# Smaller last loads, held-back loads, a cut last store and a separate last wait in a channel-attention kernel on one core

## Chip, cores and metric

The kernel runs on one core of one Trainium2 chip. The metric is the device time of one execution in microseconds; the median of the runs counts. One execution is recorded by the hardware profiler; its times are in the profile.

## What is computed

The input `x` has 1 x 384 x 384 x 384 bf16 elements (113 MB) and `w1d` has one weight (k = 1).

```python
g = jnp.einsum("bhwc->bc", x) / (H * W)      # mean of each channel over all pixels
s = _sigmoid(g * w1d[0])                      # one factor per channel
return x * s[:, None, None, :]
```

Every element is needed twice: once for the mean, before any output is known, and once to be scaled.

## The kernel before

**Layout.** The 147456 pixels are spread over the 128 partitions, 1152 rows of pixels for each partition; a row is 384 channels, 768 bytes in each partition. SBUF holds one large tile, `arena` (275 rows for each partition). "A load of n rows" brings 128 partitions x n rows.

**First pass.** The whole input is loaded once, 1152 rows. TensorE sums every row into one PSUM bank with a matrix of ones (`sum_rows`, line 272, issuing from L261). Some groups of rows stay on the chip until the second pass: some as they are ("raw"), others packed by VectorE into fewer rows (`fold`, L295 and L301, with a test on ScalarE at L332), and a few in PSUM. `N_STREAM` rows are not kept and are loaded again in the second pass. The last things loaded in the first pass are raw rows, by `take_raw` (line 466): `V`, the `LATE` pieces, `W`, `T` and `Y`. `T` and `Y` are scratch of `fold` until then. After the last row's matmul, ScalarE takes the sigmoid (L475), which gives `s_bf`.

**Second pass.** VectorE multiplies rows by `s_bf` in place (`scale`, L487; a few pieces on GpSimd), and the rows are stored (`store`, L499). Kept groups are unpacked first (`unfold`). As stores land, the rows they held come free, and rows of the stream are loaded into them (`load`, L255).

**Who sets the order.** All transfers but one tiny one are issued by SP, in one order, and the engine of each instruction waits by semaphores that `Flow` (line 21) derives from the rows read and written. SP works strictly in order: a load that waits for a store to land holds all that SP issues after it. The order of the second pass is found while the kernel is built, by a small planner (the `while True` loop at line 723). It keeps a clock `now`, a list of transfers under way (`moves`), and the free rows (`idle`; `runs()` lists the free stretches). `backlog()` is the time that the queued transfers will still take. A load is issued into the longest free stretch as soon as this line allows it:

```python
if (todo or not (landed or alongside or waiting)) and (n >= BIG or n == left or (ahead < LOW and n >= 8) or ahead < LAST):
```

Here `n` is the length of the stretch, cut to what is left, `ahead` the backlog in microseconds, `BIG` 32 rows, `LOW` 9 and `LAST` 4.

**The end.** `Flow.emit` puts everything into one critical section (`tile_critical`), and at its end SP waits for the last transfer of each of its 24 semaphore lanes (L126). Leaving the section, all engines meet; then the kernel's own end follows (L830).

Of the kernel before, what the change touches and what calls it, by code (L numbers as in the profile page):

```python
# [20 lines left out]
class Flow:  # L21
# [47 lines left out]
    def emit(self):  # L69
        nc = self.nc  # L70
        engines = {"SP": nc.sync, "ACT": nc.scalar, "PE": nc.tensor, "DVE": nc.vector, "POOL": nc.gpsimd}

        know = {e: {} for e in engines}

        def covers(k, d):
            return k.get(d.lane, 0) >= d.rank if d.dma else k.get(d.eng, -1) >= d.i

        for s in self.steps:
            k = know[s.eng]
            for d in sorted(s.deps, key=lambda d: -d.i):  # L80
                if covers(k, d):
                    continue
                s.waits.append(d)
                d.wanted = True
                for key, v in d.know.items():
                    if k.get(key, -1) < v:
                        k[key] = v
            s.know = dict(k)
            if s.dma:
                s.know[s.lane] = s.rank  # L90
            else:
                s.know[s.eng] = s.i

        count, sems = {}, {}
        for s in self.steps:
            if not s.dma and s.wanted:
                s.rank = count[s.eng] = count.get(s.eng, 0) + 1

        def sem(s):
            key = s.lane if s.dma else s.eng  # L100
            if key not in sems:
                name = f"f_{key[0]}{key[1]}" if s.dma else f"f_{key}"
                sems[key] = self.tc.alloc_semaphore(name)
            return sems[key]

        last = {}
        with self.tc.tile_critical():  # L107
            for s in self.steps:
                eng = engines[s.eng]
                waits = [(sem(d), d.rank * (16 if d.dma else 1)) for d in s.waits]  # L110
                hold = None if s.dma or s.bare or not waits else waits.pop()
                for h, v in waits:
                    eng.wait_ge(h, v)
                ins = s.emit()
                if ins is None:
                    continue
                if hold:
                    ins = ins._wait_ge(*hold)
                if s.dma:
                    ins.then_inc(sem(s), 16)  # L120
                    last.pop(s.lane, None)
                    last[s.lane] = s
                elif s.wanted:
                    ins.then_inc(sem(s), 1)
            for lane, s in last.items():
                engines[lane[0]].wait_ge(sem(s), 16 * s.rank)  # L126


@with_exitstack
def kernel(  # L130
# [11 lines left out]
    nc = tc.nc  # L142
    P = nc.NUM_PARTITIONS
    B, H, W, C = x.shape
# [16 lines left out]
    V = G0 + PAIRS * 3 * PAIR  # L161
    A = V + PAIR
    N_A = 39
    T = A + N_A
    Y = T + 2 * PIECE
# [14 lines left out]
    W = A + 3 * PIECE  # L180
# [13 lines left out]
    arena = pool.tile([P, ROWS, C], bf16, name="arena")  # L194
# [13 lines left out]
    of = out.rearrange("b h w c -> (b h w) c")  # L208
# [4 lines left out]
    def view(t, r0, n):  # L213
        return t[r0 * P : (r0 + n) * P, :].rearrange("(p r) c -> p r c", r=n)
# [193 lines left out]
    for i, bk in enumerate(banks):  # L408
        lo, hi = i * BANK, min((i + 1) * BANK, PS * C)
# [31 lines left out]
    LATE = [(W + 4, 8), (U, 8), (W + 12, 8), (W + 20, 7)]  # L441
# [8 lines left out]
    left = first - N_FIRST  # L450
# [15 lines left out]
        load(raw(a), a, n)  # L466
        sum_rows(a, n)

    for a, n in [(V, 8), *LATE, (W, 4), (T, 8), (Y, 4), (Y + 4, 3), (Y + 7, 1)]:
        take_raw(a, n)  # L470
    assert summed[0] == RPP

# [17 lines left out]
            reads=rows(a, n) + ["s_bf" if s is s_bf else "bank0"], writes=rows(a, n), after=after,  # L490
        )

    def store(at, a, n):
        r0, m = run = run_of(at)
        lo, hi = at - r0, at - r0 + n
        assert hi <= m
        return fl.add(
            "SP",
            lambda: nc.sync.dma_start(out=view(of, *run)[:, lo:hi, :], in_=arena[:, a : a + hi - lo, :]),  # L499
            reads=rows(a, hi - lo), dma=True,  # L500
        )

    def unfold(k, first):

# [88 lines left out]
    ROW, PER_LOAD, PER_STORE = 0.2267, 0.112, 0.061  # L593
    LAT, SEEN, DT = 2.0, 1.5, 0.05
    PENDING, MERGE = 24.0, 12.0
    BIG, CAP, PART, LOW, LAST = 32, 48, 16, 9.0, 4.0
    BANKS_AT = 2
    N_SPLIT = 2
    now = dve_at = 0.0
    moves, waiting, over, acts = deque(), deque(), deque(), deque()  # L600
    landed = deque()
    idle = [False] * ROWS
    todo = 0
# [35 lines left out]
    def stored(a, n):  # L639

        def f():
            for i in range(a, a + n):
                unused.discard(i)
                if not Y <= i < Y + 8:
                    idle[i] = True
        return f
# [8 lines left out]
    alongside = deque()  # L655
# [17 lines left out]
    since = None  # L673
    asked = checked = False
    stall = 0.0

    def start_group():

# [44 lines left out]
    while True:  # L723

        if dve_at <= now:
            ahead = backlog()
            can = bool(turns)
            if not can and not alongside and (ahead >= PENDING or not landed):
                can = start_group()
            if landed and (ahead < PENDING or not can):  # L730
                a, at, n, end = landed.popleft()
                scale(a, n, s=s_ps if alongside and now else s_bf)
                dve_at = now + TT(n)
                since = (a, at) if since is None else since
                if end or ahead < MERGE:
                    b, first = since
                    send(first, b, at + n - first, stored(b, at + n - first))
                    since = None
            elif can:
                f, t, then = turns.popleft()  # L740
                f()
                dve_at = now + t
                if then:
                    then()
        if alongside and alongside[0][0] <= now:
            _, a, at, n = alongside.popleft()
            store(at, a, n)
            moves.append([now + LAT, n * ROW + PER_STORE, stored(a, n)])
        while waiting and waiting[0][0] <= now:
            _, n, then, at, a, known = waiting.popleft()  # L750
            known.append(store(at, a, n))
            moves.append([now + LAT, n * ROW + PER_STORE, then])
        if not asked and not line and not turns:
            verdict()
            asked = True
        if out_rows == total and not checked:
            checked = True
            fl.add("POOL", again, reads=["odd_i", "s_bf"], writes=rows(Y, N_OVER), after=written, bare=True)
        while over and over[0][0] <= now:
            over.popleft()[1]()  # L760

        got = runs()
        if bank_at is None and len(line) <= total - BANKS_AT and got and max(got)[0] >= N_BANKED:
            a = max(got)[1]
            for i in range(a, a + N_BANKED):
                idle[i] = False
            back = arena[:, a : a + PS, :].rearrange("p r c -> p (r c)")
            for i, bk in enumerate(banks):
                lo, hi = i * BANK, min((i + 1) * BANK, PS * C)
                copy_bank(bk[:, 0 : hi - lo], back[:, lo:hi], [("bank", i)], rows(a, PS))  # L770
            for lo, hi, at, cell in PARTS:
                copy_bank(at, arena[:, a + N_BANKED - 1, lo:hi], [], rows(a + N_BANKED - 1, 1) + [cell])
            bank_at = (a, now + 5.0)
            got = runs()

        if got and todo < N_STREAM:
            n, a = max(got)
            left = N_STREAM - todo
            left -= run_of(left - 1)[0]
            n = min(n, CAP, left)  # L780
            ahead = backlog()
            if (todo or not (landed or alongside or waiting)) and (n >= BIG or n == left or (ahead < LOW and n >= 8) or ahead < LAST):

                lo = N_STREAM - todo - n
                load(lo, a, n)
                for i in range(a, a + n):
                    idle[i] = False
                parts = [(a + e, lo + e, f - e, f == n) for e, f in split(n, PART)]
                todo += n
                moves.append([now + LAT, n * ROW + PER_LOAD, lambda parts=parts: landed.extend(parts)])  # L790

        if moves and moves[0][0] <= now:
            moves[0][1] -= DT
            if moves[0][1] <= 0:
                over.append((now + SEEN, moves.popleft()[2]))
        else:
            stall += DT
        if not (alongside or moves or waiting or over or landed or line or turns) and todo == N_STREAM:
            break
        now += DT  # L800
# [34 lines left out]
```

## Time and profile before

| | us |
|---|---|
| runs | 720.6, 720.0, 720.54 |
| median | 720.54 |
| profiled execution, its own time | 720.05 |
| its span (first to last instruction of the record) | 718.3 |

| engine | busy us | share of the span |
|---|---|---|
| VectorE (DVE) | 485.6 | 68% |
| TensorE (PE) | 213.0 | 30% |
| ScalarE (ACT) | 122.1 | 17% |
| GpSimd (POOL) | 10.2 | 1% |
| DMA queue of SP, share of 16 engines' span | | 98.9% |

The page gives busy times over the whole span, cut into 40 slices of 18 us. PE and ACT work almost only in the first 270 us, the summing pass; DVE works in both. The windows view cuts any stretch of the span into pieces of its own. In it a row is: window in us, its length, then busy time of PE, PE weight load, DVE, ACT and POOL (with the count of instructions that overlap it), the granted TensorE clock, the share of the 16 DMA engines that is busy, and the GB/s that they move. A share slightly over 1 comes from transfers that are counted where they begin. In the timeline view a row is: start in us, duration, engine, line, operation, and in brackets the idle time before it and what ended it.

### The profile page before, as it was taken

To read this page: it belongs to the slowest core of one execution; us is meant where nothing else is said; L and a number is where in the kernel's file an instruction comes from. 1 tells how busy PE (TensorE), PEld (TensorE's weight loads), DVE (VectorE), ACT (ScalarE), POOL (GpSimd) and SP (SyncE) were. 2 spreads that over 40 slices of the span, in tenths; PEclk is the share of its full clock that TensorE was granted. 3 is DMA by queue.
4 is the path that set the end of the run, shared out by engine and by line. 5 is a ranking of instruction groups with operands and counts; after the bars stand their busy time and mean duration, and the time that the engine had idled before them with its cause. 6 is when DMAs were issued, how large, how long until landed. Compare 5 with 4: busy or idle time off the path is not lost.

```text
span 718.3 us, 2042 instructions
## 1 busy us (share of the span) xinstructions
PE 213.0 (30%) x1186; PEld 0.3 (0%) x3; DVE 485.6 (68%) x454; ACT 122.1 (17%) x101; POOL 10.2 (1%) x7
## 2 busy tenths in 40 slices
PE   4776977997868770000000000000000000000000
PEld 0000000000000000000000000000000000000000
DVE  4606270639896819998997999996991999005640
ACT  3604160426674610000002000000000000000000
POOL 0000000000000005000000000000000000000000
PEclk9989889999999995555555555555555555555555
DMA  9999999999999989999999999999999999999997
GB/s 372 443 422 444 434 431 418 447 428 424 428 426 428 425 343 359 413 424 430 425 434 429 433 443 424 435 426 437 434 431 432 443 431 426 436 429 431 447 421 307
DMA packets 21181, 303.30 MB, mean 422 GB/s; under 512 B 2354, under 2 KB 2738, under 8 KB 9010
## 3 DMA queue, kind: packets, MB, share of 16 engines
q1 hardware_dynamic: 21168, 303.18, 98.9%
q8 instruction: 4, 0.07, 0.0%
q14 instruction: 7, 0.06, 0.0%
q10 hardware_dynamic: 2, 0.00, 0.0%
HBM read 189.92 MB, written 113.25 MB: 422 GB/s over the span
## 4 chain that ended last, share of the span: by engine, by line
DMA 54%; DVE 27%; PE 7%; ACT 3%; another core or an unknown queue 2%; POOL 1%; SPq 1%; issue 1%; DVEq 0%; ACTq 0%
DMA arena<-in_x_dram 38%; DVE arena L487 19%; DMA out_dram<-arena 16%; PE bank L261 7%; DVE arena L295 6%; DVE arena L301 3%; ACT arena L332 2%; POOL arena L487 1%; SPq L255 1%; ACT arena L405 1%; SPq L499 0%; ACT s_bf L475 0%; ACT bank L479 0%; ACT bank L405 0%
## 5 line engine op out<-in xcount | busy, mean ns | idle before, releaser
L487 DVE TENSOR_TENSOR arena<-arena,s_bf 128x1536 bf16<-128x1536 bf16 (+9 forms) x100 | 231.0, 2345 | 84.4 <-DMA arena<-in_x_dram 68.2
L261 PE MATMUL bank<-arena,ones 128*128 128x384 bf16 x1151 | 207.1, 341 | 46.7 <-DMA arena<-in_x_dram 46.2
L295 DVE TENSOR_SCALAR arena<-arena 128x1536 uint16<-128x1536 uint16 (+3 forms) x240 | 142.9, 644 | 111.4 <-DMA arena<-in_x_dram 94.9
L332 ACT ACTIVATE arena<-arena 128x3072 uint16<-128x3072 uint16 (+1 forms) x40 | 108.0, 2700 | 111.0 <-DVE arena L295 111.0
L301 DVE TENSOR_TENSOR arena<-arena 128x1536 uint16<-128x1536 uint16 (+2 forms) x100 | 109.3, 1093 | 7.9 <-PE bank L261 4.0
L557 PE MATMUL bank<-odd,ones 128*128 128x1 bf16 x1 | 0.2, 185 | 313.8 <-DVE odd L552 313.8
L405 ACT COPY arena<-bank 128x512 uint32<-128x512 uint32 (+3 forms) x9 | 4.4, 497 | 107.9 <-DMA out_dram<-arena 107.6
L487 POOL TENSOR_TENSOR arena<-arena,s_bf 128x1536 bf16<-128x1536 bf16 (+1 forms) x3 | 10.0, 3351 | 269.4 <-ACT bank L479 269.4
L487 DVE TENSOR_TENSOR arena<-arena,bank 128x1536 bf16<-128x1536 bf16 (+3 forms) x8 | 9.4, 1250 | 0.0
L405 ACT COPY bank<-arena 128x512 uint32<-128x512 uint32 (+3 forms) x9 | 4.1, 494 | 26.3 <-PE bank L261 26.2
L332 ACT ACTIVATION_READ_ACCUMULATOR arena<-arena 128x1 f32 x40 | 7.5, 186 | 0.0
L261 PE MATMUL bank<-zeros,ones 128*128 128x384 bf16 x32 | 5.5, 326 | 0.0
L475 ACT ACTIVATE s_bf<-bank,w_sc 128x384 bf16<-128x384 f32 x1 | 0.6, 580 | 13.9 <-PE bank L261 13.9
L275 PE MATMUL bank<-arena,ones 128*128 128x384 bf16 x1 | 0.5, 477 | 7.2 <-DMA arena<-in_x_dram 7.2
L803 ACT ACT_TABLE_LOAD x1 | 1.3, 1283 | 0.7 <-PEq L819 0.7
L362 DVE TENSOR_SCALAR w_sc<-bank 128x1 f32<-128x1 f32 x1 | 0.2, 159 | 1.1 <-PE bank L357 1.1
L352 DVE MEMSET ones<- 128x128 bf16 x1 | 0.2, 165 | 1.0 <-SPq L107 1.0
L357 PE MATMUL bank<-w_bf,ones 1*128 1x1 bf16 x1 | 0.2, 178 | 2.2 <-DMA w_bf<-in_w1d_dram 2.2
L557 PEld LDWEIGHTS bank<-odd,ones 128*128 128x128 bf16 x1 | 0.1, 103 | 572.9 <-DVE odd L552 572.9
L561 DVE CAST odd_i<-bank 128x1 int32<-128x1 f32 x1 | 0.2, 157 | 0.3 <-PE bank L557 0.3
L479 ACT COPY bank<-s_bf 128x192 uint32<-128x192 uint32 x1 | 0.3, 323 | 0.0
L547 DVE TENSOR_REDUCE worst<-seen 128x1 f32<-128x40 f32 x1 | 0.2, 188 | 0.0
(8 smaller groups left out, 0.9 us busy)
## 6 DMA issues: line engine op xcount, KB each, us to landing
arena<-in_x_dram SPq DMA_DIRECT2D x16, 4608.0 KB, 29.9
out_dram<-arena SPq DMA_DIRECT2D x9, 3072.0 KB, 24.1
out_dram<-arena SPq DMA_DIRECT2D x5, 4608.0 KB, 35.8
arena<-in_x_dram SPq DMA_DIRECT2D x7, 2304.0 KB, 19.8
arena<-in_x_dram SPq DMA_DIRECT2D x14, 1152.0 KB, 17.0
arena<-in_x_dram SPq DMA_DIRECT2D x5, 3072.0 KB, 15.2
arena<-in_x_dram SPq DMA_DIRECT2D x18, 768.0 KB, 8.9
arena<-in_x_dram SPq DMA_DIRECT2D x2, 4512.0 KB, 29.4
```

The costliest lines, as they stand in the source:

```text
L255: lambda: nc.sync.dma_start(out=arena[:, a : a + hi - lo, :], in_=view(xf, *run)[:, lo:hi, :]),
L261: return pe.add_instruction(mybir.InstMatmult(name=nc.get_next_instruction_name(), ins=[pe.lower_ap(rhs), pe.lower_ap(ones[:])], outs=[pe. ...
L275: return nc.tensor.matmul(acc, lhsT=ones[:], rhs=arena[:, i, :], start=first, stop=last)
L295: lambda: nc.vector.tensor_scalar(out=dst, in0=src, scalar1=s0, scalar2=s1, op0=op0, op1=op1),
L301: "DVE", lambda: nc.vector.tensor_tensor(out=dst, in0=a, in1=b, op=op), reads=reads, writes=writes
L332: lambda: nc.scalar.activation(out=y, in_=y, func=ACTF.Copy, accum_out=seen[:, 2 * k + i : 2 * k + i + 1]),
L405: "ACT", lambda: nc.scalar.copy(dst.bitcast(u32), src.bitcast(u32)), reads=reads, writes=writes
L475: lambda: nc.scalar.activation(out=s_bf[:], in_=acc, func=ACTF.Sigmoid, scale=w_sc[:, 0:1]),
L479: "ACT", lambda: nc.scalar.copy(s_ps.bitcast(u32), s_bf[:].bitcast(u32)), reads=["s_bf"], writes=["bank0"]
L487: lambda: vec.tensor_tensor(out=v, in0=v, in1=s[:, None, :].to_broadcast([P, n, C]), op=Op.mult),
L557: lambda: nc.tensor.matmul(votes, lhsT=ones[:], rhs=odd[:], start=True, stop=True),
L803: nc.scalar.preload_act_table(ACTF.Sigmoid)
```

## The change

Four edits, all to the order and the cutting of transfers:

1. The last loads of the first pass: `T` in two loads of 4 rows in place of one of 8, `Y` in 4, 2, 2 rows in place of 4, 3, 1.
2. The planner holds a load back while three things hold together: a store was issued since the last load (`storing`), fewer than `MANY` = 32 rows are free in all, and the backlog is at least `SHORT` = 5 us. In the order that results, the first eight loads of the second pass stay as they were, and later ones differ in size and place; the last loads are of 48, 48, 8 and 43 rows where they were of 48, 36, 22 and 43.
3. The last store (output rows at `at` = 0, 43 rows) is cut: its first `N_LAST` = 6 rows go as three transfers of 13, 51 and 64 partitions, the other 37 rows as one transfer of all partitions.
4. The wait for the transfer issued last is taken out of the list of 24 and put into a critical section of its own, after the first.

```diff
@@ Flow.emit
-            for lane, s in last.items():
-                engines[lane[0]].wait_ge(sem(s), 16 * s.rank)
+            ends = list(last.values())
+            for s in ends[:-1]:
+                engines[s.eng].wait_ge(sem(s), 16 * s.rank)
+        with self.tc.tile_critical():
+            engines[ends[-1].eng].wait_ge(sem(ends[-1]), 16 * ends[-1].rank)
@@
-    for a, n in [(V, 8), *LATE, (W, 4), (T, 8), (Y, 4), (Y + 4, 3), (Y + 7, 1)]:
+    for a, n in [(V, 8), *LATE, (W, 4), (T, 4), (T + 4, 4), (Y, 4), (Y + 4, 2), (Y + 6, 2)]:
         take_raw(a, n)
@@
-    def store(at, a, n):
+    def store(at, a, n, p0=0, p1=P):
...
-            lambda: nc.sync.dma_start(out=view(of, *run)[:, lo:hi, :], in_=arena[:, a : a + hi - lo, :]),
+            lambda: nc.sync.dma_start(
+                out=view(of, *run)[p0:p1, lo:hi, :], in_=arena[p0:p1, a : a + hi - lo, :]
+            ),
...
+    def store_last(at, a, n):
+        for p0, p1 in zip(LAST_CUTS, LAST_CUTS[1:]):
+            store(at, a, N_LAST, p0, p1)
+        return store(at + N_LAST, a + N_LAST, n - N_LAST)
@@ planner
+    MANY, SHORT = 32, 5.0
+    N_LAST, LAST_CUTS = 6, (0, 13, 64, P)
+    storing = True
...
             store(at, a, n)
+            storing = True
...
-            known.append(store(at, a, n))
+            known.append((store if at else store_last)(at, a, n))
+            storing = True
...
-            if (todo or not (landed or alongside or waiting)) and (n >= BIG or n == left or (ahead < LOW and n >= 8) or ahead < LAST):
+            behind = storing and sum(m for m, _ in got) < MANY and ahead >= SHORT
+            if not behind and (todo or not (landed or alongside or waiting)) and (n >= BIG or n == left or (ahead < LOW and n >= 8) or ahead < LAST):
+                storing = False
```

## Prediction

> **What bounds the kernel now.** I read the page's slices first, then the queue table, then windows of busy time over the second half, over the hand-over between the two passes, and over the last microseconds.
>
> ```profile
> DMA  9999999999999989999999999999999999999997
> GB/s 372 443 422 444 434 431 418 447 428 424 428 426 428 425 343 359 413 424 430 425 434 429 433 443 424 435 426 437 434 431 432 443 431 426 436 429 431 447 421 307
> q1 hardware_dynamic: 21168, 303.18, 98.9%
> HBM read 189.92 MB, written 113.25 MB: 422 GB/s over the span
> ...
> 290.00:712.00 422.00, 0.18 (x1) 0.10 (x1) 319.25 (x233) 4.37 (x9) 0.00 (x0) 0.50 1.01 432
> ```
>
> The DMA engines bound it. The last row (window; busy time of PE, weight load, DVE, ACT, POOL; clock; DMA share; GB/s) says that from 290 to 712 us they have no idle time: share 1.01, 432 GB/s, while DVE is busy 319 of 422 us. So an edit in this stretch gains only if it removes bytes, and an order of loads and stores can only lose, by leaving the engines empty. Three places are not full: the first slice, slices 15 and 16 (343 and 359 GB/s, where the summing pass ends and the scaling pass begins) and the last (307). The change touches the last two.
>
> A row of the arena is 128 x 768 B = 98.3 KB, so 0.228 us at 432 GB/s. The 21168 packets are 147 transfers of 144: 128 data packets, 8 for each of 16 engines, and one closing packet for each engine.
>
> The hand-over:
>
> ```profile
> 262.00:264.00 2.00, 1.83 (x12) 0.00 (x0) 0.00 (x0) 0.00 (x0) 0.00 (x0) 1.00 0.99 411
> 264.00:266.00 2.00, 1.16 (x9) 0.00 (x0) 0.00 (x0) 0.00 (x0) 0.00 (x0) 1.00 0.85 337
> 266.00:268.00 2.00, 2.00 (x13) 0.00 (x0) 0.00 (x0) 0.00 (x0) 0.00 (x0) 1.00 0.20 76
> 268.00:270.00 2.00, 0.75 (x5) 0.00 (x0) 0.60 (x2) 0.90 (x2) 0.20 (x1) 1.00 0.00 0
> 270.00:272.00 2.00, 0.00 (x0) 0.00 (x0) 2.00 (x3) 0.00 (x0) 2.00 (x1) 0.82 0.53 197
> ...
> 263.20 1.95 PE L261 MATMUL bank<-arena,ones 128*128 128x384 bf16 x11 [0.17 <-DMA arena<-in_x_dram]
> 265.99 2.76 PE L261 MATMUL bank<-arena,ones 128*128 128x384 bf16 x16 [0.84 <-DMA arena<-in_x_dram]
> 268.78 0.58 ACT L475 ACTIVATE s_bf<-bank,w_sc 128x384 bf16<-128x384 f32 x1 [13.93 <-PE bank L261]
> ```
>
> PE stands 0.84 us until the 8-row load into T has landed, then runs the last 16 rows (8, 4, 3, 1) without a wait, 2.76 / 16 = 0.173 us each, and the sigmoid starts at its end. The last loads land while PE is still behind: here PE ends last, not DMA.
>
> The end:
>
> ```profile
> 712.00:712.50 0.50, 0.00 (x0) 0.00 (x0) 0.00 (x0) 0.00 (x0) 0.00 (x0) 0.50 0.46 198
> 712.50:713.00 0.50, 0.00 (x0) 0.00 (x0) 0.00 (x0) 0.00 (x0) 0.00 (x0) 0.50 0.16 66
> 713.00:713.50 0.50, 0.00 (x0) 0.00 (x0) 0.00 (x0) 0.00 (x0) 0.00 (x0) 0.50 0.01 0
> 713.50:714.00 0.50, 0.00 (x0) 0.00 (x0) 0.00 (x0) 0.00 (x0) 0.00 (x0) 0.50 0.31 132
> 714.00:714.50 0.50, 0.00 (x0) 0.00 (x0) 0.00 (x0) 0.00 (x0) 0.00 (x0) 0.50 0.00 0
> 714.50:715.00 0.50, 0.00 (x0) 0.00 (x0) 0.00 (x0) 0.00 (x0) 0.00 (x0) 0.50 0.15 66
> 715.00:715.50 0.50, 0.00 (x0) 0.00 (x0) 0.00 (x0) 0.00 (x0) 0.00 (x0) 0.50 0.15 66
> 715.50:718.30 2.80, 0.00 (x0) 0.00 (x0) 0.00 (x0) 0.00 (x0) 0.00 (x0) 0.50 0.00 0
> ...
> L126 SPq EVENT_SEMAPHORE x12: 17/28/28, 692.2 to 716.7; - x12
> SPq L830 <- PEq L830: 0.8, 2, 0.6
> ```
>
> Packets count in the window where they start. The last store moves 43 x 768 = 33 KB packets. After 713.5 there are four: two (132 GB/s x 0.5 us = 66 KB), then one and one. Their time, 0.31 x 16 x 0.5 = 2.48 us for two, is 1.24 us each: 27 GB/s, a sixteenth of the full rate. So two of the 16 engines are not slow but late, by about 3 us, and end near 716.4, when the other fourteen, whose last packets start by 712.5, end at about 713.2 in the middle. Then SP's last wait passes at 716.7 and the span ends at 718.3.
>
> **The change part by part.** *Last loads 4, 4, 4, 2, 2.* Before, T lands at 265.95. Now its first half lands 4 x 0.228 = 0.91 us sooner, at 265.04; PE is free at 263.20 + 1.95 = 265.15 and sums it by 265.84; the second half is there at about 266.0 (one closing packet more) and summed by 266.7. Y's four rows land at 266.9, summed by 267.6; two more at 267.4, summed by 267.95; the last two at about 267.9, summed by 268.3. PE ended at 268.75: -0.45 us. PE now waits for DMA at nearly every piece, so I take -0.4. Bounds: 0, if splitting delays each landing by as much as it saves, and -0.55, when PE ends 0.35 us after the last landing. One more load is issued on SP; the engines have queued work then (share 0.99), which hides it. The whole second pass is a full queue behind the sigmoid, so this goes through to the end.
>
> *Load behind a store.* I read the issue order of both kernels. Second-pass rows stay 780 loaded and 1152 stored; before in 30 + 60 transfers, after in 29 + 60, not counting the three cut pieces. From the second load of 10 rows on, loads merge and move behind stores (for example 24 + 10 rows where there were 10 and 24 with a store between). A load waits for stores to land, and every store behind it on SP waits too; the DVE steps that read it wait as well. Bytes equal, engines full: 0, as long as the queue never runs empty. I tallied DVE's steps and the transfers along both orders, with rows of this kind:
>
> ```profile
> L487 DVE TENSOR_TENSOR arena<-arena,s_bf 128x6144 bf16<-128x6144 bf16 x26 | 85.6, 3352 | 52.7 <-DMA arena<-in_x_dram 52.7
> L487 DVE TENSOR_TENSOR arena<-arena,s_bf 128x4608 bf16<-128x4608 bf16 x31 | 78.7, 2556 | 12.2 <-DMA arena<-in_x_dram 11.5
> L487 DVE TENSOR_TENSOR arena<-arena,s_bf 128x1536 bf16<-128x1536 bf16 x19 | 18.2, 958 | 0.7
> ```
>
> (3.35 us for 16 rows, 2.56 for 12, 0.96 for 4: 0.155 + 0.2 a row.) Before, the tightest place is the 48-row store near 525 us, which by this tally comes about 2 us ahead of an empty queue. After, it is a 48-row store near 506, with 1 to 2 us to spare. So 0 is my value; the bounds are +3 us (the tally wrong by as much as it could be) and -0.5 (fewer small packets and disturbances).
>
> *Last store cut.* Six of its 43 rows go as 13, 51 and 64 partitions, the other 37 as before. In this trace every transfer has 128 partitions and gives each engine the same number of packets. 64 partitions give each engine 4 packets of 6 x 768 = 4.6 KB (0.171 us at 27 GB/s) where it had 8. The other 64 partitions, 13 and 51, can't be split evenly over 16. If a late engine gets none of them it saves 4 x 0.171 = 0.68 us; with one packet 0.51. If pieces are spread evenly all the same, 0; if the 51 go onto few engines, those end later: on three (51 = 3 x 17) they carry 17 + 1 + 4 = 22 packets for 8, 14 x 0.171 = 2.4 us more, so 713.2 + 2.4 = 715.6, just under the late two's 715.8; on one, 713.2 + 8 = 721. I take -0.55, nearest to the equal split that all 147 transfers show. SP issues three more transfers while 8 us and more of stores are queued, so their issue is hidden; were that cover gone, they would cost some 0.33 us each.
>
> [...]
>
> *Last wait apart.* SP's other 23 waits and the section's meeting of all engines now come while the last store is still moving; only one wait, and a short section of SP alone, follow. Of the 1.6 us from 716.7 to 718.3, L830's meeting (0.8) stays, so at most 0.8 can go, and 0 at least; SP still has a branch, a drain and two no-ops, so I take -0.15. Queued behind the 23 waits is only the end of the section, for which no work waits.
>
> Sum: -0.4 + 0 - 0.55 - 0.15 = -1.1 us. The profiled execution took 720.05 us, half a microsecond below the median of 720.54 and at the bottom of the runs (720.0 to 720.6); against it 718.95, against the median **719.4**, 0.15% less. A measurement of this kernel tells about 0.2%, 1.4 us, from no change.
>
> **The rivals.** *A, slower: a late engine takes part of the 51.* The 17 packets of one engine fall on one that is already 3 us late. For it: if shares must be equal, 51 can only go onto three engines or one, and the chance that two late ones of 16 miss three is 78/120. Against: nothing in the profile numbers the engines. That engine ends at 716.4 + 2.4: total -0.4 + 2.4 - 0.15 = +1.85, **722.4**. It ends last as soon as the heavy engine is over 0.2 us late, and undoes the other gains (0.55) from about 1.3 us of lateness on. Chance 0.14.
>
> *B: the queue runs empty near 506 us.* For it: the spare of 1 to 2 us is smaller than the tally's drift, up to 2 us. Against: in that place before, with hardly more to spare, share and GB/s stay full. A gap of 2 us gives **721.4**. Chance 0.08.
>
> *C: the late engines are less late.* Their 3 us came somewhere in the scaling pass, and the order changes there from about 315 us on. A third less is -1 us more: **718.3**; as likely it grows, and part of that lies in the forecast's own range. Chance 0.2.
>
> *D: the cut does nothing*, since 13 and 51 partitions are spread nearly evenly. -0.55 and **720.0**. [...] Chance 0.1.
>
> **How the numbers follow.** The forecast has 0.48, its own range is 718.7 to 720.2. Faster by over 0.2% means below 719.1: a third of the forecast (0.17) and nearly all of C (0.19), 0.36. Slower means above 722.0: most of A and a little of B, 0.14. Between, 0.50. The range leaves out A's upper part and C's far end: 718.2 to 721.4.
>
> **What would show it.** Sigmoid start near 268.4 and PE waits before the last pieces: the first step. Share 1.01 in windows from 290 to 700, with no window of 2 us near 505 below 0.9: no B. At the end, some three engines ending with the late two, about 715.7, and packets of 28 KB in the last window: the cut; one engine alone for over 2 us at 718: A. SP's last wait less than 1.6 us before the span's end: the last edit. I am wrong if the sigmoid does not move, or if the two late engines lie elsewhere than at 3 us.

## Result and the profile after

The changed kernel takes 722.15 us (median of 22 runs, 721.06 to 723.8), the kernel before, run beside it, 720.48 (22 runs, 719.81 to 722.54). The ratio is 1.0024 [1.0019, 1.003]: **1.7 us slower**. The profiled execution took 721.79 us with a span of 719.9; that of before 720.05 and 718.3.

The page after (the DMA slices, GB/s in them, and the queue of SP: packets, MB, share):

```profile
DMA  9999999999999989999999999999999999999996
GB/s 373 441 424 440 433 430 425 437 430 428 426 427 414 425 344 376 411 429 423 432 435 424 428 438 427 439 433 437 426 436 428 439 426 437 432 433 432 437 418 278
q1 hardware_dynamic: 21328, 303.18, 98.8%
```

The bytes are the same and the middle looks the same. The last slice fell from 307 to 278 GB/s; no other differs from before by more than 17. The packets grew by 160, from 147 x 144. The number of full transfers is still 147 (one more load in the first pass, one fewer in the second), so the 160 belong to the three pieces: 128 for the data, 32 that close a piece on an engine. 32 = 13 + 3 + 16. Spread over all engines, the pieces would have closed 48 times. So the pieces of 13, 51 and 64 partitions went to 13, 3 and 16 engines, and the trace has as many landings of each.

Windows after, over the second pass and around 506 us (columns as in the prediction):

```profile
290.00:712.00 422.00, 0.18 (x1) 0.10 (x1) 319.52 (x232) 4.38 (x9) 0.00 (x0) 0.50 1.01 431
500.00:504.00 4.00, 0.00 (x0) 0.00 (x0) 4.00 (x2) 0.00 (x0) 0.00 (x0) 0.50 1.02 442
504.00:508.00 4.00, 0.00 (x0) 0.00 (x0) 3.93 (x7) 0.00 (x0) 0.00 (x0) 0.50 1.02 442
508.00:512.00 4.00, 0.00 (x0) 0.00 (x0) 3.93 (x4) 0.00 (x0) 0.00 (x0) 0.50 1.00 433
```

The engines are full throughout, also where the tally had only 1 to 2 us to spare. No gap came with the held-back loads.

The hand-over after, in the timeline (PE and ACT):

```profile
263.45 2.66 PE L264 MATMUL bank<-arena,ones 128*128 128x384 bf16 x15 [0.16 <-DMA arena<-in_x_dram]
266.30 2.39 PE L264 MATMUL bank<-arena,ones 128*128 128x384 bf16 x12 [0.19 <-DMA arena<-in_x_dram]
...
268.73 0.58 ACT L478 ACTIVATE s_bf<-bank,w_sc 128x384 bf16<-128x384 f32 x1 [13.62 <-PE bank L264]
```

PE's wait of 0.84 us for the eight rows has become one of 0.19 us for the second four and a short one inside the second row: its 12 matmuls span 2.39 us, 0.3 more than at 0.173 each. The sigmoid starts only 0.05 us earlier than in the profile of before, but ACT's idle time ahead of it, in the bracket, is 13.62 us for 13.93; the experiments come back to this.

The last microseconds after (windows of half a microsecond, then SP's last wait and the meeting of the engines):

```profile
713.50:714.00 0.50, 0.00 (x0) 0.00 (x0) 0.00 (x0) 0.00 (x0) 0.00 (x0) 0.50 0.13 57
714.00:714.50 0.50, 0.00 (x0) 0.00 (x0) 0.00 (x0) 0.00 (x0) 0.00 (x0) 0.50 0.53 227
714.50:715.00 0.50, 0.00 (x0) 0.00 (x0) 0.00 (x0) 0.00 (x0) 0.00 (x0) 0.50 0.13 57
715.00:715.50 0.50, 0.00 (x0) 0.00 (x0) 0.00 (x0) 0.00 (x0) 0.00 (x0) 0.50 0.40 171
715.50:716.00 0.50, 0.00 (x0) 0.00 (x0) 0.00 (x0) 0.00 (x0) 0.00 (x0) 0.50 0.00 0
716.00:716.50 0.50, 0.00 (x0) 0.00 (x0) 0.00 (x0) 0.00 (x0) 0.00 (x0) 0.50 0.26 114
716.50:717.00 0.50, 0.00 (x0) 0.00 (x0) 0.00 (x0) 0.00 (x0) 0.00 (x0) 0.50 0.00 0
717.00:717.50 0.50, 0.00 (x0) 0.00 (x0) 0.00 (x0) 0.00 (x0) 0.00 (x0) 0.50 0.13 57
...
L128 SPq EVENT_SEMAPHORE  x1: 17/17/17, 718.8 to 718.8; - x1
SPq L848 <- PEq L848: 0.8, 2, 0.6
```

A packet of the last 37 rows is 28.4 KB, so one that starts in a window shows as 57 GB/s. Before, the last one started by 715.5. Now two start after 716.0 and one after 717.0, and SP's last wait passes at 718.8 instead of 716.7. The loss lies here, in what ends last. The landings in the trace (one for each engine: the moment at which its share of a transfer is reported done, some 0.35 us after its last packet) of the 51-partition piece and of the last store:

```
                       landings, us
51 partitions, after   707.07  708.39  709.14
last 37 rows, after    eleven 712.58 to 714.64;  715.78  716.15  716.55  717.86  718.57
```

Three engines took the 51 packets, 17 each; call them heavy. The first was done with them at 707.07, the others 1.3 and 2.1 us later. At the end, too, one of these three stands at 716.15 and two at 717.86 and 718.57, 1.7 and 2.4 us later; 715.78 and 716.55 fit the two engines that were late before. Stringing packets into engines by their times, one heavy engine moved its 22 small packets in 3.92 us, 0.178 each, close to the 0.171 of the prediction. The others took longer for as many: single packets of 4608 B lasted 0.33 to 0.69 us.

### The profile page after: what moved, and what is told of

It is laid out like the page before. It is cut to its first block, busy times and chain, and to the rows that moved or that the text cites. A ratio compares the mean times of both kernels' runs of the same rounds, so it can differ in the third digit from the quotient of the medians.

```text
span 719.9 us, 2055 instructions
## 1 busy us (share of the span) xinstructions
PE 212.6 (30%) x1186; PEld 0.3 (0%) x3; DVE 485.8 (67%) x453; ACT 122.2 (17%) x101; POOL 10.2 (1%) x7
## 4 chain that ended last, share of the span: by engine, by line
DMA 60%; DVE 22%; PE 6%; ACT 2%; another core or an unknown queue 2%; SPq 1%; issue 1%; DVEq 0%
DMA arena<-in_x_dram 44%; DVE arena L490 17%; DMA out_dram<-arena 16%; PE bank L264 6%; DVE arena L298 4%; ACT arena L335 2%; DVE arena L304 2%; SPq L258 1%; ACT s_bf L478 0%; ACT bank L408 0%; DVEq L113 0%; SPq L848 0%; SPq L107 0%
## 5 line engine op out<-in xcount | busy, mean ns | idle before, releaser
L490 DVE TENSOR_TENSOR arena<-arena,s_bf 128x4608 bf16<-128x4608 bf16 (+9 forms) x99 | 231.0, 2367 | 84.5 <-DMA arena<-in_x_dram 68.6
```

Source lines behind the costliest of these rows:

```text
L490: lambda: vec.tensor_tensor(out=v, in0=v, in1=s[:, None, :].to_broadcast([P, n, C]), op=Op.mult),
```

## Experiments

Each kernel is the kernel before with the edit named, unless it says otherwise, and is compared with the kernel before on the same chip.

| kernel | this, us | before, us | difference | ratio [95%] |
|---|---|---|---|---|
| e1, edit 1 | 720.03 | 720.20 | -0.17 | 0.9997 [0.9988, 1.0006] |
| e2, edit 2 | 720.49 | 720.20 | +0.29 | 1.0003 [0.9994, 1.0012] |
| e3, edit 3 | 722.39 | 720.20 | **+2.19** | 1.0036 [1.0022, 1.005] |
| e4, edit 4 | 720.13 | 720.20 | -0.07 | 1.0001 [0.9992, 1.001] |
| e5, edits 1, 2, 4 | 719.79 | 720.29 | -0.50 | 0.9993 [0.9983, 1.0002] |
| e12, e5 again | 719.77 | 720.38 | -0.61 | 0.9993 [0.9984, 1.0002] |
| e16, edits 1, 4 | 719.99 | 720.37 | -0.38 | 0.9996 [0.9987, 1.0005] |
| e6, halves | 721.45 | 720.29 | +1.16 | 1.0015 [1.0006, 1.0024] |
| e7, 51 moved | 721.03 | 720.29 | +0.74 | 1.0008 [0.9999, 1.0017] |
| e8, 16 pieces | 723.29 | 720.29 | +3.0 | one run |
| e9, by rows only | 720.33 | 720.38 | -0.05 | 1.0002 [0.9993, 1.0011] |
| e11, even and odd | 720.72 | 720.38 | +0.34 | 1.0005 [0.9996, 1.0015] |
| e10, 42 rows as halves | 728.88 | 720.38 | **+8.5** | one run |
| e13, 42 rows even and odd | 720.67 | 720.37 | +0.3 | one run |
| e14, halves to even and odd | 729.02 | 720.37 | **+8.65** | one run |
| e15, even and odd to halves | 720.88 | 720.37 | +0.5 | one run |

### Each edit alone

**e1**, the last loads:

```diff
-    for a, n in [(V, 8), *LATE, (W, 4), (T, 8), (Y, 4), (Y + 4, 3), (Y + 7, 1)]:
+    for a, n in [(V, 8), *LATE, (W, 4), (T, 4), (T + 4, 4), (Y, 4), (Y + 4, 2), (Y + 6, 2)]:
```

> The kernel before with the last loads alone changed (4, 4, 4, 2, 2 rows). Theory 1 (the step works as predicted, and in the changed kernel's profile it was hidden by loads that landed 0.3 us later for another reason): 0.2 to 0.45 us faster, sigmoid near 268.4 us. Theory 2 (an extra load and its closing packets delay the last landing by what the split saves): no change, within 0.1 us, sigmoid near 268.75 us.

**e2**, the held-back loads:

```diff
+            behind = storing and sum(m for m, _ in got) < MANY and ahead >= SHORT
-            if (todo or ...
+            if not behind and (todo or ...
```

> The kernel before with the planner's held-back loads alone. Theory 1 (the engines stay full, so the order is worth nothing by itself): within 0.5 us of before, share 1.0 in every window of 2 us near 505 us, the latest engine ends within 0.5 us of 716.3. Theory 2 (the order makes single engines later or empties the queue): 1 us or more slower, and the latest engine ends after 717 us.

**e3**, the last store with `store_last` and `N_LAST, LAST_CUTS = 6, (0, 13, 64, P)`:

> The kernel before with the cut of the last store alone (13, 51, 64 partitions of the first 6 rows). Theory 1 (the 51 partitions go onto three engines, and their 4.6 KB packets take far more than 0.171 us, so these engines end last): 1.5 to 2.5 us slower, the last packets start near 717 us. Theory 2 (the cut does what was predicted, and the loss of the whole change comes from the order of the loads): 0.4 to 0.7 us faster.

**e4**, the last wait in its own section:

```diff
+            for s in ends[:-1]:
+                engines[s.eng].wait_ge(sem(s), 16 * s.rank)
+        with self.tc.tile_critical():
+            engines[ends[-1].eng].wait_ge(sem(ends[-1]), 16 * ends[-1].rank)
```

> The kernel before with the last wait alone set apart. Both theories: 0.1 to 0.2 us faster; the last wait passes 1.4 to 1.5 us before the span's end where it was 1.6 us. A rival: the second section costs what the first one saves, and the time stays within 0.1 us.

The cut alone costs 2.2 us, more than the whole change; the other three stay within what the measurement can tell (e1's -0.17 us lies between its two theories, e4's -0.07 fits its rival). For these, the traces say more than the times. The hand-over in the timeline, of e1 and then of e2, which keeps the old loads:

```profile
263.40 2.66 PE L261 MATMUL bank<-arena,ones 128*128 128x384 bf16 x15 [0.15 <-DMA arena<-in_x_dram]
266.25 2.39 PE L261 MATMUL bank<-arena,ones 128*128 128x384 bf16 x12 [0.19 <-DMA arena<-in_x_dram]
...
268.68 0.58 ACT L475 ACTIVATE s_bf<-bank,w_sc 128x384 bf16<-128x384 f32 x1 [13.63 <-PE bank L261]
```

```profile
266.27 2.76 PE L261 MATMUL bank<-arena,ones 128*128 128x384 bf16 x16 [0.82 <-DMA arena<-in_x_dram]
...
269.07 0.58 ACT L475 ACTIVATE s_bf<-bank,w_sc 128x384 bf16<-128x384 f32 x1 [13.91 <-PE bank L261]
```

The start of the sigmoid itself differs from execution to execution by what came before: 268.78 to 269.81 in the 13 profiles with the old loads (before was the earliest), 268.64 to 268.87 in the five with the new ones (e1, e5, e12, e16, after). The bracket is steadier. It gives ACT's idle time since its last work, far ahead of the edit: 13.88 to 13.95 us with the old loads (13.93 before), 13.62 to 13.64 with the new ones. That is a gain of 0.28 us, and the starts of PE's matmuls in the trace show where it comes from. Where nothing holds them up they are 0.16 us apart. Before has one gap of 1.16 us, ahead of the eight rows of `T`; e1 has three, of 0.23, 0.51 and 0.45 us, ahead of the halves of `T` and the four rows of `Y`. Beyond the 0.16 they add up to 1.00 and 0.70 us.

In e4 the last landing is at 717.01 and the span ends at 718.37, 1.36 us later; before it was 716.70 and 718.26, 1.56 us. All five profiles with this edit have 1.36 us here, and all thirteen without it 1.56 or 1.57: a gain of 0.20 us. SP's last wait in e4:

```profile
L128 SPq EVENT_SEMAPHORE  x1: 17/17/17, 717.2 to 717.2; - x1
```

It lies 1.2 us before the end of the span, where it was 1.6; but it now passes 0.2 us after the landing and not at once, so the landings tell the gain.

### The change without its cut, and without the rule for loads

**e5** and **e12** are the changed kernel with the last store whole; **e16** is e5 with the rule for loads off:

```diff
-            known.append((store if at else store_last)(at, a, n))
+            known.append(store(at, a, n))
@@ e16 only
-            behind = storing and sum(m for m, _ in got) < MANY and ahead >= SHORT
+            behind = False
```

> The changed kernel with the last store whole (the other three edits stay). Theory 1 (the cut is the whole loss, the other edits are worth about -0.3, +0.2 and -0.1 us): 0.1 to 0.5 us faster than before, the latest engine ends near 716.3 us. Theory 2 (the edits only lose together, by making more engines late): slower than before by 0.5 us or more.

> The changed kernel with the last store whole, again, since its first measurement (0.5 us faster) was inside its interval. Theory 1 (three small gains and no loss): 0.2 to 0.6 us faster than before. Theory 2 (the first measurement was chance): within 0.15 us of before.

> The kernel before with the last loads and the separate wait alone (no cut, no held-back loads). Theory 1 (held-back loads are worth nothing): 0.3 to 0.6 us faster than before, as with them (0.5 and 0.6). Theory 2 (they are worth the difference between the single edits and the three together): 0.1 to 0.3 us faster.

Without the cut the change gains 0.50 and 0.61 us, about the 0.28 of the loads and the 0.20 of the wait. Twice alike, but each interval reaches 1.0002, so the gain is likely and not proven. Putting the cut's 2.2 on top gives the 1.7 of the whole change. e16 differs from e5 and e12 by 0.1 to 0.2 us: the order of the loads is worth nothing that these runs can tell from 0. The ends of e3 and e5, side by side in windows of 2 us (the first two rows e3, the last two e5):

```profile
714.00:716.00 2.00, 0.00 (x0) 0.00 (x0) 0.00 (x0) 0.00 (x0) 0.00 (x0) 0.50 0.26 114
716.00:718.00 2.00, 0.00 (x0) 0.00 (x0) 0.00 (x0) 0.00 (x0) 0.00 (x0) 0.50 0.10 43
```

```profile
714.00:716.00 2.00, 0.00 (x0) 0.00 (x0) 0.00 (x0) 0.00 (x0) 0.00 (x0) 0.50 0.08 33
716.00:718.00 2.00, 0.00 (x0) 0.00 (x0) 0.00 (x0) 0.00 (x0) 0.00 (x0) 0.50 0.00 0
```

e5 ends as before did; in e3 packets start after 716, as in the changed kernel. Two heavy engines end last there too, landing at 717.71 and 718.06; next comes a late one at 717.42, itself slowed in its small packets (one took 0.81 us).

### Which part of the cut: the count, the place or the small packets

**e6** cuts the 6 rows in two even pieces, `6, (0, 64, P)`: every engine gets the same 4 + 4 packets, none is heavy. **e7** moves the piece of 51 to the middle, `6, (0, 30, 81, 96, P)`. **e9** keeps the 6 rows whole, `6, (0, P)`: only a transfer more. **e11** takes the even and then the odd partitions:

```diff
+        for p0 in (0, 1):
+            store(at, a, N_LAST, p0, P, 2)        # slices [p0:p1:by]
```

> The kernel before, the first 6 rows of the last store cut into two pieces of 64 partitions in place of 13, 51 and 64. Theory 1 (cutting as such costs nothing, uneven pieces do): within 0.3 us of before, all 4.6 KB packets near 0.178 us. Theory 2 (small packets of a cut store are slow wherever they go): 1 us or more slower.

> The kernel before with the first 6 rows of the last store as partitions 0 to 29, 30 to 80, 81 to 95 and 96 to 127: the piece of 51 starts at 30 in place of 13, and three engines still have 22 packets in all, ten or more others 5. In the cut of the change one of the three engines took 0.178 us a packet and two took 0.24 to 0.28. [...] Theory Q (any piece on three engines is slow, or a heavy engine is one of the late ones): 1.5 us or more slower, as with the cut of the change.

> The kernel before, the last store cut by rows alone: 6 rows and 37 rows, both over all 128 partitions. Theory 1 (small packets are slow only where an engine reads other partitions than in a store of all 128): all 4.6 KB packets near 0.178 us, time within 0.3 us of before. Theory 2 (small packets beside the 28 KB packets of other engines are slow anywhere, or their places in HBM are): packets of 0.3 us and more among those of the late engines, 0.5 to 1.2 us slower.

> The kernel before, the first 6 rows of the last store as two pieces of 64 partitions again, but the even and the odd partitions in place of the lower and the upper half. Sizes, counts and engines are those of e6. Theory 1a (an engine's share of a store of 128 is eight partitions next to each other; by parity it stays inside them): within 0.3 us of before. Theory 1b (the shares of 128 lie otherwise, so parity moves engines into others' partitions too): slower as e6. Theory 2 (two pieces cost what they cost wherever they lie): 1 to 1.3 us slower as e6.

**e8** cuts them into pieces of 15, 14, ... 1 and 8 partitions, which tells the engines apart by the pieces they have no part in:

> The kernel before with the first 6 rows of the last store in 16 pieces of 15, 14, 13, down to 1, and 8 partitions. [...]

The queue's line on the pages of e7, e8 and e9:

```profile
q1 hardware_dynamic: 21345, 303.18, 98.9%
```

```profile
q1 hardware_dynamic: 21424, 303.18, 98.8%
```

```profile
q1 hardware_dynamic: 21312, 303.18, 99.0%
```

Over 21168 they have 177, 256 and 144 packets. Less the 128 of data, 49 = 15 + 3 + 15 + 16 for pieces of 30, 51, 15 and 32; 128 = 15 + 14 + ... + 1 + 8; and 16. The sums are those of the largest divisor up to 16 of the partitions of each piece.

How long the packets of the last two transfers took, from the trace (128 of each size):

```
                        rows cut off             the rest
            size, B     mean ns   max ns     size, B  mean   max
before      -           -         -          33024    1222   1222
after        4608       219       692        28416    1056   1418
e3           4608       212       809        28416    1054   1092
e6 halves    4608       221       805        28416    1053   1053
e7           4608       195       718        28416    1055   1241
e9 by rows   4608       178       178        28416    1053   1053
e11 ev./odd  4608       178       178        28416    1053   1053
e10 halves   32256      2018      3864
e13 ev./odd  32256      1194      1194
e14          32256      2012      3706
e15          32256      1194      1194
```

Even halves are slow (+1.16) although no engine is heavy; small packets over all partitions are not (e9); nor are those of half the partitions, if they are every second one (e11: all take 0.178 us, and its +0.34 us is not told from 0). So neither the small packets nor a count of partitions makes the cut slow, but a contiguous range does. In e6 the late engines pay for it: from the store before to the end of their eight small packets they took 2.0 and 2.2 us, in e9 1.4.

e7 is 0.74 us slower than before, half of theory Q's 1.5, with an interval that just reaches 0.9999. Its piece of 51 was done at 706.78, 707.26 and 708.29, so one of the three engines was still slowed; the move cured one of two. The late engines were slowed as well: three engines end nearly together, landing at 717.17, 717.24 and 717.29, the heavy one and the two late ones.

e8 also answers who is late. The landings of its small pieces show two engines later than the rest in the piece of 5 (710.51, 711.22), one in the piece of 4 (710.7) and none in the piece of 3 (706.62 to 707.08). So neither late engine has a share in the piece of 3. That its three engines are the three of a 51 no trace shows, since none numbers the engines. But in the changed kernel the two late engines, which landed their share of the store ahead at 706.25 and 706.96, landed theirs of the piece of 13 at 706.44 and 707.16. Another 17 packets of 0.178 us from there would land at 709.47 and 710.19, an estimate that takes an engine's pieces in the order of issue, and the last of the 51 landed at 709.14. By that no late engine carries the 51. They come late to the last stores without being slower there: in the profile of before all 128 packets of the last store took 1.222 us, theirs too. Why they are late was not tried.

### The same with large packets, and SBUF told from HBM

**e10** and **e13** repeat e6 and e11 with 42 of the 43 rows (`N_LAST = 42`), so that the effect has room.

> The kernel before, 42 of the last store's 43 rows as two pieces of 64 partitions (the last row over all 128): the disputed cost by itself, seven times as large. Theory 1 (a piece of 64 partitions makes engines read the same places in SBUF in pairs, and one of a pair waits): 3 to 10 us slower, many of the 32 KB packets take far more than 1.2 us. Theory 2 (a cut costs a fixed amount for each piece): about as e6, 1 to 1.5 us slower.

> The kernel before, 42 of the last store's 43 rows as even and as odd partitions, the large form of the piece that cost little. Both theories: within 0.7 us of before, all 32 KB packets near 1.19 us; if the cost grew with the rows as in the halves (8.5 us), parity would be no cure.

A half of the partitions is a half in SBUF and a half of the addresses in HBM. **e14** reads halves of SBUF and writes to the even and odd places of HBM, **e15** the reverse (so these output rows are permuted, and the two kernels serve the timing alone):

```diff
+        halves, parity = (slice(0, 64), slice(64, P)), (slice(0, P, 2), slice(1, P, 2))
+        for here, there in zip(halves, parity):   # e15: zip(parity, halves)
...      out=view(of, *run)[there, lo:hi, :], in_=arena[here, a : a + hi - lo, :]
```

> 42 of the last store's 43 rows: the lower half of the partitions of SBUF is written to the places of the even partitions in HBM, the upper half to those of the odd (so these output rows are permuted). Theory S (the slow packets come from what engines read in SBUF at the same time): about 8 us slower, as the plain halves, 32 KB packets of 2 us and more. Theory H (they come from the places in HBM): within 0.7 us of before.

> The reverse: even partitions of SBUF to the lower half of the places in HBM, odd partitions to the upper half (these output rows are permuted). Theory S: within 0.7 us of before, all packets near 1.19 us. Theory H: about 8 us slower.

The last stores in windows, of e10, e13, e14 and e15 in this order:

```profile
704.00:712.00 8.00, 0.00 (x0) 0.00 (x0) 0.00 (x0) 0.00 (x0) 0.00 (x0) 0.50 1.04 265
...
716.00:718.00 2.00, 0.00 (x0) 0.00 (x0) 0.00 (x0) 0.00 (x0) 0.00 (x0) 0.50 0.99 226
718.00:726.00 8.00, 0.00 (x0) 0.00 (x0) 0.00 (x0) 0.00 (x0) 0.00 (x0) 0.50 0.25 59
```

```profile
704.00:712.00 8.00, 0.00 (x0) 0.00 (x0) 0.00 (x0) 0.00 (x0) 0.00 (x0) 0.50 1.04 450
...
716.00:718.00 2.00, 0.00 (x0) 0.00 (x0) 0.00 (x0) 0.00 (x0) 0.00 (x0) 0.50 0.01 3
```

```profile
704.00:712.00 8.00, 0.00 (x0) 0.00 (x0) 0.00 (x0) 0.00 (x0) 0.00 (x0) 0.50 0.98 259
...
718.00:726.00 8.00, 0.00 (x0) 0.00 (x0) 0.00 (x0) 0.00 (x0) 0.00 (x0) 0.50 0.35 79
```

```profile
704.00:712.00 8.00, 0.00 (x0) 0.00 (x0) 0.00 (x0) 0.00 (x0) 0.00 (x0) 0.50 1.00 432
...
716.00:718.00 2.00, 0.00 (x0) 0.00 (x0) 0.00 (x0) 0.00 (x0) 0.00 (x0) 0.50 0.02 6
```

A share of 1.04 with 265 GB/s says that all engines are busy and move little more than half: each packet takes longer, 2.02 us on average for 1.19. Read by the share alone, this window looks as good as that of e13. The slowness goes with the halves of SBUF (e10, e14) and not with the halves of HBM (e15): **a store that reads a contiguous half of the partitions is held up where SBUF is read**. These are single runs, but 8 us is far more than the 1.4 us over which the runs of before beside them spread. Nor is it only the packets of the halves that suffer: of the store ahead of them, which covers all partitions, the packets that were still to come on late engines took up to 1.57 us in e10, 1.55 in e14 and 1.19 in e7, where in e13 and e15 every one takes 0.63. So a packet is slowed by what other engines read beside it. The six traces agree (means of 0.221, 2.018 and 2.012 us in e6, e10 and e14, 0.178 and 1.194 in e11, e13 and e15): halves of SBUF slow, even and odd not. Which engine reads which partitions, and whether engines hold each other up in pairs, no trace shows. e7, whose piece of 51 lies on both sides of 64, was cured by half (+0.74 us for +2.19), so the halves are not the whole account.

## Why the prediction was wrong

**Step by step.** The bound was read rightly: the second pass is full before and after, and what was lost was lost in the last slice.

- *Last loads*, -0.4 us: -0.28 by ACT's idle time ahead of the sigmoid. Right, a little smaller, with PE waiting ahead of three of the five pieces; that the sigmoid would start near 268.4 was wrong, since the profile of before was an early one (268.78, where others with its loads have 268.88 to 269.81).
- *Load behind a store*, 0: +0.29 alone and -0.1 to -0.2 inside the change, neither to be told from 0. Right as far as these runs can tell.
- *Last wait apart*, -0.15: -0.20 from the last landing to the end of the span. Right in the trace; in the time (-0.07) it drowns.
- *Last store cut*, -0.55: **+2.2**. This is the step that failed. Its -0.55 was the author's estimate from 0.171 us a packet; no run shows it, and the cut alone cost 2.19 us (e3). The prediction got the count right: "on three (51 = 3 x 17) they carry 17 + 1 + 4 = 22 packets for 8, 14 x 0.171 = 2.4 us more, so 713.2 + 2.4 = 715.6, just under the late two's 715.8". It priced each packet at the rate of transfers that cover all partitions. One of the three engines kept that rate and ended at 716.15; for the other two, the 51 partitions of the lower half cost 1.3 and 2.1 us more, and the end moved to 718.57. There was no room for an error of this kind, since the plan put the heavy engines 0.2 us under the late ones. Nor did the late engines gain the forecast 0.5 us: from their landing of the store ahead of it to the last landing they took 9.53 and 9.59 us, before 9.74 and 9.75. Their five small packets took 1.12 and 1.20 us where 5 x 0.178 = 0.89.

The sum of the three right steps, -0.55 as forecast and -0.48 by the traces (with 0 for the order of the loads), is about what e5 and e12 measured; with +2.2 it gives the +1.7 of the result.

**Rivals.** *A* came near in time (722.4 for 722.15) by luck, since the mechanism is another: by the landings no late engine has a share of the 51 (the estimate above), and in the changed kernel the heavy engines and the late ones end apart. *B* did not occur. *C*: the two latest engines landed their share of the store ahead of the cut at 706.25 and 706.96, before at 706.66 and 706.96, not a third less late (and its price, 1 us off 719.4, is 718.4 where the prediction has 718.3). *D* is out: the pieces went to 13, 3 and 16 engines. Nor does an even spread make a cut free: with 42 of the 43 rows as halves the kernel took 8.5 us longer than with one piece. What was missing among the rivals was that a packet's time depends on the partitions that its neighbours read (16.9 KB of a whole store took 0.63 us in e13 and e15, up to 1.57 beside the halves in e10).

## What to carry to other kernels

Cut a store by its rows or by every second partition, not by ranges of partitions: a cut of 6 rows over all partitions cost nothing (-0.05 us), by every second partition 0.3 us, not told from 0, the same rows as halves 1.2 us, 42 rows as halves 8.5. When a cut is to relieve a late engine, price both the packets that the other engines take over and their duration in the new shape, and leave more room than 0.2 us. A full DMA share does not mean full rate: read GB/s beside it (in e10 a share of 1.04 at 265 GB/s, in e13 at 450).

## What the runs showed of the hardware

- In the last stores, with no range of partitions among them, all packets of one size take the same time, to the nanosecond, whether the store covers all 128 partitions or every second one: 0.178 us for 4.6 KB, 1.053 for 28.4, 1.194 for 32.3, 1.222 for 33.0 (before, e9, e11, e13, e15). Packets of contiguous halves take up to 3.86 us for 32.3 KB, packets of a whole store beside them up to 1.57 for 16.9 KB in place of 0.63, and it is the SBUF side that holds them up (mean 2.012 us with halves of SBUF in e14, 1.194 with halves of HBM in e15).
- The pieces tried were closed as often as the largest divisor up to 16 of their partitions adds up to: 32 times in the changed kernel (13 by 13 engines, 51 by 3 and 64 by 16, by the landings too), 49 in e7, 128 in e8.
- In the store ahead of the last, two engines land some 3 us after the others (3.05 and 3.35 us in the profile of before) without being slower per packet there. In most other profiles one to three more are 0.9 to 2.4 us late.
